# Whole rows and TensorE transposes for the first pair's q and k, forget gates on 96 partitions

## The chip, the cores and the metric

The kernel runs on one core of a Trainium2 chip. The metric is the device time of one execution in microseconds (us); the times before are the median of 3 runs.

## The reference

Three layers follow each other in fp32. The change touches the start of the first.

```python
# attention with forget gates: B, H, S, D = 4, 8, 576, 64
scores = (q @ k.transpose(0, 1, 3, 2)) / np.sqrt(D)
cum = np.cumsum(np.log(np.clip(f, 1e-4, 1.0)), axis=-1)
scores = np.where(causal, -1e9, scores + cum[:, :, :, None] - cum[:, :, None, :])
attn = softmax(scores)                       # causal masks the future
x = (attn @ v).transpose(0, 2, 1, 3).reshape(B * S, H * D)   # 2304 x 512

# a feed-forward layer, 512 -> 2048 -> 512, with a quadratic activation g
x = g(x @ w_in) @ w_out

# a top-1 mixture of 8 experts, 512 -> 1024 -> 512
out[n] = gate[n] * (relu(x[n] @ w1[e[n]]) @ w2[e[n]])
```

## The kernel before

The kernel is written as processes (Python generators) that a planner, the class `Order`, runs against a clock of its own: each step names an engine, a cost, a function that issues its instructions, and a rank; the lowest rank that is ready on an engine goes first. The order in which the functions are called is the order of the program on each engine's queue, so the planner's costs and due times decide the order, while on the chip each instruction waits for its real inputs. What a planner's gap on TensorE leaves open, `keep_warm` (L746 and after) fills with matmuls on the identity; every second turn issues one, and the first turn comes when `setup` is over, which costs 3000 ns on the planner's clock.

Attention goes over 16 pairs of heads. A pair has five units (blocks of 128 queries, in the order 4, 3, 2, 1, 0; block 4 holds the last 64 queries of both heads, and `corner` on GpSimd lays its q out in `qz`). A `unit` takes one of two score banks in PSUM (`SR` and `SRx`, two slots each), TensorE writes the scores into it and, for the first four pairs, adds the decays to them by a second set of matmuls (`sums`): pair 0 takes them from `cum` itself, pairs 1 to 3 from `parts`, which `sum_parts` makes from `cum`, later pairs by adding rows that have gone through DRAM (`rows`). Then `head` reads the bank on VectorE (L606), takes the exponential on ScalarE (L611), scales on GpSimd (L623) and turns the probabilities on TensorE (L637). `weighted` multiplies them with v.

The decays come from `forget_rows`: the gates are loaded four times, into 4 x 32 partitions of `cum` (L366), clamped (L370), their logarithm is taken (L372), scaled by -8 (L374) and summed along the sequence by a scan (L378). Before the scan it waits for `first_kt`, that is, for k of pair 0 to be turned.

q and k of a pair come by `load` (L411), four DMAs each on SP's queue, in pieces of 32 elements, and `turned` turns them by one VectorE transpose each (L464). Pair 1's DMAs wait, on the planner's clock, for pair 0's k. All of `attention` waits for the event `sums_there` before its first unit.

Beside attention the planner runs the first half of the feed-forward layer as soon as blocks of x are there, and prepares its weights in 16 pieces (`float64_piece`: L846 the DMA, L855 to L872 the steps on ScalarE, VectorE and GpSimd), whose earliest times stand in `FIRST_WEIGHTS`. Then come the second half and the experts, which are matmuls in a steady order.

Of the kernel before, what the change touches and what calls it, by code (L numbers as in the profile page):

```python
# [18 lines left out]
P = 128  # L19
# [18 lines left out]
NQK = 3  # L38
NP_ = 8
NSUM = 4  # L40
FIRST_WEIGHTS = [6000.0 + 2700.0 * n for n in range(5)] + [20500.0 + 5200.0 * n for n in range(11)]
PACE = 8500.0
WARM_FROM, WARM = 1500.0, 0.6
# [148 lines left out]
def dve(n, fn, prio=5.0, fast=False):  # L192
    return Use("DVE", 144 + n * (0.6 if fast else 1.05), fn, prio)
# [31 lines left out]
def kernel(  # L225
# [71 lines left out]
    statt = ap.tile([P, 10, 10], F32, name="stat")  # L297
    stats = [statt[:, n] for n in range(10)]

    cum = ap.tile([P, S], F32, name="cum")  # L300
    parts = ap.tile([P, S], F32R, name="parts")
    pick = ap.tile([NH, P], F32, name="pick")
    picks = ap.tile([P, P * NSUM], F32R, name="picks")
    past = [ap.tile([P, n], F32, name=f"past{n}") for n in (512, S)]
# [4 lines left out]
    p_b, sr_b, t_b, x_b, pt_b, pt4_b, xt_b = (  # L309
        Buffers(NP_), Buffers(4), Buffers(2), Buffers(1), Buffers(4), Buffers(1), Buffers(2))  # L310
    rows_there = Event()
    clamped, scaled_ok, first_kt = Event(), Event(), Event()
    sums_there = Event()
    parts_there = Event()
    raw_ok = {(i, n): Event() for i in range(NP) for n in "qk"}
# [13 lines left out]
    for b in range(B):  # L329
        for n in range(b * S // TB, ((b + 1) * S - 1) // TB + 1):  # L330
            xs_ok[n].n += NPAIR
    raws, qkt, cms, vs, pt, pt4, xts = {}, {}, {}, {}, {}, {}, {}

    def setup():
        make_identity(nc, ident)
# [20 lines left out]
    def forget_rows():  # L356


        got = yield (p_b, 3)
        low, rest, mids = (ap.tile([P, S], F32, tag="P", name=n, bufs=NP_)  # L360
                           for n in ("low", "rest", "mids"))
        go(sum_parts(rest, mids, got))

        def loads():
            for p0 in range(0, P, NH):
                nc.scalar.dma_start(cum[p0:p0 + NH], f.rearrange("b h s -> (b h) s"))  # L366
        yield Use("DVE", 400, lambda: (nc.vector.memset(quarter, 0.25), nc.vector.memset(low, -8.0)), 0)
        go(ln_table())
        yield dma(4 * NH * S * 4, loads, 0, "ACT", k=4)
        yield dve(S, lambda: nc.vector.tensor_scalar(cum, cum, 1e-4, 1.0, ALU.max, ALU.min), 0, True)  # L370
        done(clamped)
        yield act(S, lambda: nc.scalar.activation(cum, cum, AF.Ln), 0)  # L372
        go(exp_table())
        yield dve(S, lambda: nc.vector.tensor_scalar(cum, cum, -8.0, None, ALU.mult), 0, True)  # L374
        done(scaled_ok)
        yield first_kt

        yield dve(S, lambda: nc.vector.tensor_tensor_scan(cum, low, cum, 0.0, ALU.max, ALU.add), 0)  # L378
        done(sums_there)
        yield dma(NH * S * 4, lambda: nc.sync.dma_start(rows, cum[:NH]), 2)  # L380
        done(rows_there)

    def sum_parts(rest, mids, got):
        mids = mids.bitcast(F32R)
        yield sums_there
        yield act(S, lambda: nc.scalar.copy(parts, cum), 0.9)
        yield dve(S, lambda: nc.vector.tensor_tensor(rest, cum, f32(parts), ALU.subtract), 0.9)
        yield act(S, lambda: nc.scalar.copy(mids, rest), 0.9)
        yield Use("ACT", 700, lambda: nc.scalar.copy(parts[NH:2 * NH], rest[NH:2 * NH]), 0.9)
        yield dve(S, lambda: nc.vector.tensor_tensor(rest, rest, f32(mids), ALU.subtract), 0.9)  # L390
        yield Use("ACT", 700, lambda: nc.scalar.copy(parts[2 * NH:3 * NH], rest[2 * NH:3 * NH]), 0.9)
        give(p_b, got)
        done(parts_there)

    def ln_table():
        yield 600.0
        yield Use("ACT", 1400, lambda: nc.scalar.activation(tiny, quarter, AF.Ln), 0)
# [4 lines left out]
    def load(i, n):  # L402
        b, hp = divmod(i, NPAIR)
        h0 = 2 * hp

        def put(src, n):
            t = ap.tile([P, S // 32, 32], F32, tag="raw" + n, name=f"raw{n}{i}", bufs=2)
            for j in range(2):
                for dh in range(2):
                    p0 = 64 * j + 32 * dh  # L410
                    nc.sync.dma_start(  # L411
                        t[p0:p0 + 32],
                        src[b, h0 + j, :, 32 * dh:32 * dh + 32].rearrange(
                            "(tb t) d -> t tb d", t=32))
            return t
        g = yield (raw_b[n], 1)
        if i == 1:
            yield raw_ok[0, "k"]
        elif i:
            yield sums_there  # L420
        t = yield dma(P * S * 6, lambda: put({"q": q, "k": k}[n], n),
                      4 if i > 1 else 0.5, k=4)
        raws[i, n] = (t, g)
        done(raw_ok[i, n])

    def loadv(i):
        b, hp = divmod(i, NPAIR)
# [14 lines left out]
    def prep():  # L442

        for i in range(NP):
            for n in "qk":
                go(load(i, n))
        for i in range(NP):
            g = yield (qk_b, 1)
            qkt[i] = ([ap.tile([P, S], F32, tag=f"{n}t{g[0]}", name=f"{n}t{i}") for n in "qk"],
                      qz[g[0]], g)  # L450
            go(turned(i, "q"))
            go(turned(i, "k"))

    def turned(i, n):

        pr = PREP if i else 0
        yield raw_ok[i, n]
        if i == 0:
            yield clamped if n == "q" else scaled_ok
        r, g = raws.pop((i, n))  # L460
        r = r.rearrange("p a b -> p (a b)")
        (qt, kt), z, _ = qkt[i]
        t = qt if n == "q" else kt
        yield dve(S, lambda: nc.vector.transpose(t, r), pr)  # L464
        give(raw_b[n], g)
        done(qk_ok[i])
        if i == 0 and n == "k":
            done(first_kt)
        if n == "q":
            def corner():  # L470
                for j in range(2):
                    p = slice(64 * j, 64 * j + 64)
                    nc.gpsimd.tensor_copy(z[p, p], qt[p, 512:S])
            yield Use("POOL", 500, corner, pr)
            done(qk_ok[i])
# [60 lines left out]

    def unit(i, c, started):

        yield qk_ok[i]
        heads = (None,) if c == 4 else (0, 1)  # L540
        gp_ = yield (p_b, len(heads))
        sl = yield (sr_b, ((0, 1), (2, 3)))
        bank = SR[sl[0] // 2]
        done(started)
        (qt, kt), z, _ = qkt[i]
        w = P * (c + 1) if c < 4 else S

        def scores():
            if c == 4:
                for n in range(2):  # L550
                    nc.tensor.matmul(bank[:, n, :S // 2], z, kt[:, S // 2 * n:S // 2 * (n + 1)],  # L551
                                     start=True, stop=i >= NSUM)
                return
            for j in range(2):
                p = slice(64 * j, 64 * j + 64)
                nc.tensor.matmul(bank[:, j, :w], qt[p, P * c:P * c + P], kt[p, :w],  # L556
                                 start=True, stop=i >= NSUM)

        def sums():
            n3 = 3 * NH  # L560
            if i == 0:
                for n in range(2):
                    if c == 4:
                        nc.tensor.matmul(bank[:, n, :S // 2], pick,
                                         cum[:NH, S // 2 * n:S // 2 * (n + 1)], start=False, stop=True)
                    else:
                        p = slice(64 * n, 64 * n + NH)
                        nc.tensor.matmul(bank[:, n, :w], ident[p, 65 * n:65 * n + 1].to_broadcast(
                            [NH, P]), cum[p, :w], start=False, stop=True)
                return  # L570
            if c == 4:
                for n in range(2):
                    nc.tensor.matmul(bank[:, n, :S // 2], picks[:n3, P * i:P * i + P],
                                     parts[:n3, S // 2 * n:S // 2 * (n + 1)], start=False, stop=True)
                return
            for j in range(2):
                h = 64 * (2 * i + j)
                nc.tensor.matmul(bank[:, j, :w], picks[:n3, h:h + 1].to_broadcast([n3, P]),
                                 parts[:n3, :w], start=False, stop=True)
        yield Use("PE", max(440, 1.72 * w), scores, 0.8, full=0.8)  # L580
        done(s_done[i])
        if i < NSUM:
            yield parts_there if i else sums_there
            yield Use("PE", mm(w if c < 4 else S // 2, 2) if i else 1.72 * w, sums, 0.8)
        yield cm_ok[i, c]
        st = stats[(5 * i + SEQ.index(c)) % len(stats)]
        summed, scaled = Event(len(heads)), Event()
        left = Event(len(heads))
        for n, j in enumerate(heads):
            p = ap.tile([P, S], F32, tag="P", name=f"P{i}_{j}{c}", bufs=NP_)  # L590
            go(head(i, j, c, p, [gp_[n]], bank, st, summed, scaled, left))
        yield left
        give(sr_b, sl)
# [1168 lines left out]
```

## Time and profile before

| | us |
|---|---|
| median of 3 runs | 851.88 |
| lowest and highest | 850.98, 852.60 |
| the profiled execution | 852.66 |
| its span, first to last instruction | 851.0 |
| TensorE busy | 833.0 |
| VectorE busy | 443.7 |
| ScalarE busy | 360.4 |
| GpSimd busy | 303.5 |

Busy times are of the profiled execution. PE is TensorE, PEld its loading of weights, DVE is VectorE, ACT ScalarE, POOL GpSimd, SP the engine whose queue issues most DMAs. Matmuls overlap, so a busy TensorE isn't one at its peak. An fp32 matmul stands in the trace as two instructions.

### The profile page before, as it was taken

How to read it: one execution, taken by the hardware profiler on the slowest of the kernel's cores; microseconds unless marked ns; L12 is line 12 of the kernel's file. 1: busy time of each engine (PE TensorE's matmuls, PEld its weight loads, DVE VectorE, ACT ScalarE, POOL GpSimd, SP SyncE). 2: the span in 40 equal slices, each digit the busy share in tenths (PEclk: the TensorE clock that was granted, in tenths of full speed). 3: DMA queues.
4: the chain of work that ended last, by engine and by line, in shares of the span. 5: the costliest groups of instructions: out<-in, count | busy, mean ns of one | idle time of the engine just before them, and what ended most of it. 6: DMA issues, size and time to landing. Idle time of an engine off the chain costs nothing.

```text
span 851.0 us, 14093 instructions
## 1 busy us (share of the span) xinstructions
PE 833.0 (98%) x4886; PEld 661.1 (78%) x4886; DVE 443.7 (52%) x1081; ACT 360.4 (42%) x845; POOL 303.5 (36%) x410
## 2 busy tenths in 40 slices
PE   8999999999999999999999999999999999999997
PEld 5656666877787798888788888888998888887685
DVE  6877886555645537665755345466544521212021
ACT  5677676556556635443543342423333211102110
POOL 3657886555445534444442122212210033000000
PEclk9999999999999999999999999999999999999999
DMA  9889786565324146234422135664432111631220
GB/s 165 167 158 217 173 192 130 138 121 121 112 73 130 43 161 104 74 111 137 146 76 76 62 111 161 195 197 125 145 120 75 49 50 50 248 124 50 99 75 26
DMA packets 152152, 101.89 MB, mean 120 GB/s; under 512 B 102883, under 2 KB 122083, under 8 KB 152081
## 3 DMA queue, kind: packets, MB, share of 16 engines
q1 hardware_dynamic: 148624, 95.30, 41.8%
q0 software_dynamic: 3120, 5.27, 2.1%
q8 instruction: 39, 0.64, 0.3%
q10 hardware_dynamic: 336, 0.43, 0.2%
q14 instruction: 33, 0.26, 0.1%
HBM read 76.86 MB, written 24.49 MB: 119 GB/s over the span
## 4 chain that ended last, share of the span: by engine, by line
PE 86%; DVE 4%; POOL 3%; DMA 3%; issue 2%; ACT 1%; SPq 0%; ACTq 0%; POOLq 0%; DVEq 0%
PE hm L917 12%; PE hr L917 12%; PE hp L917 10%; PE accp L1051 7%; PE accr L1051 6%; PE accBr L1051 6%; PE accm L1063 6%; PE accBm L1063 6%; PE SR L556 4%; PE T L637 3%; PE X L677 3%; PE accBp L1051 2%; PE gt L1267 1%; PE U L730 1%; PE SR L551 1%
## 5 line engine op out<-in xcount | busy, mean ns | idle before, releaser
L939 POOL TENSOR_TENSOR glr<-gr,ghr 128x512 fp32r<-128x512 f32 x36 | 48.2, 1338 | 148.8 <-PE accBr L1051 69.1
L917 PE MATMUL hr<-rx,wb 128*128 128x512 f32 (+1 forms) x384 | 89.6, 367 | 0.0
L623 POOL TENSOR_SCALAR P<-P,stat 128x512 f32<-128x512 f32 (+3 forms) x128 | 74.3, 594 | 40.1 <-DVE stat L619 20.8
L917 PE MATMUL hm<-mx,wm 128*128 128x512 f32 (+1 forms) x336 | 87.0, 379 | 0.0
L611 ACT ACTIVATE P<-P,stat 128x512 f32<-128x512 f32 (+3 forms) x128 | 71.3, 559 | 29.0 <-DVE stat L606 28.0
L948 DVE SCALAR_TENSOR_TENSOR glm<-hm,ghm 128x512 fp32r<-128x512 f32 x36 | 24.8, 689 | 103.5 <-PE accBm L1063 68.4
L947 ACT ACTIVATE ghm<-hm 128x512 fp32r<-128x512 f32 x36 | 21.6, 599 | 132.9 <-PE accBm L1063 120.7
L917 PEld LDWEIGHTS hr<-rx,wb 128*128 128x128 f32 x384 | 65.7, 188 | 13.1
L917 PEld LDWEIGHTS hm<-mx,wm 128*128 128x128 f32 x336 | 61.0, 188 | 14.9 <-issue 3.4
L939 POOL TENSOR_TENSOR glp<-gp,ghp 128x512 fp32r<-128x512 f32 x36 | 48.6, 1350 | 57.8 <-ACT ghp L938 31.9
L1051 PE MATMUL accp<-ghp,wa 128*128 128x256 f32 (+1 forms) x384 | 68.9, 307 | 0.0
L1051 PEld LDWEIGHTS accp<-ghp,wa 128*128 128x128 f32 x384 | 53.7, 190 | 6.0 <-issue 1.8
L637 PE MATMUL T<-ident,P 128*128 128x128 f32 x320 | 52.2, 279 | 3.3 <-POOL P L623 2.7
L606 DVE CUSTOM_DVE_ANT_0 P<-SR,cm 128x512 f32<-128x512 f32 (+3 forms) x92 | 43.2, 486 | 23.3 <-PE SR L556 18.3
L637 PEld LDWEIGHTS T<-ident,P 128*128 128x128 f32 x320 | 36.6, 140 | 17.9 <-POOL P L623 8.6
L933 DVE SCALAR_TENSOR_TENSOR gr<-tr 128x512 f32<-128x512 f32 x36 | 24.8, 689 | 47.1 <-POOL glr L939 27.1
L657 ACT COPY pt<-T 128x512 f32<-128x512 f32 (+2 forms) x96 | 35.2, 391 | 33.0 <-PE T L637 32.3
L1051 PE MATMUL accr<-ghr,wb 128*128 128x512 f32 (+1 forms) x160 | 47.0, 375 | 0.0
L929 ACT ACTIVATE tr<-hr,quarter 128x512 f32<-128x512 f32 x36 | 24.8, 688 | 51.9 <-PE hr L917 24.6
L1051 PE MATMUL accBr<-ghr,wb 128*128 128x512 f32 (+1 forms) x160 | 46.5, 372 | 0.0
L1063 PE MATMUL accm<-wm,ghm 128*128 128x512 f32 x144 | 46.3, 394 | 0.0
L1063 PE MATMUL accBm<-wm,ghm 128*128 128x512 f32 x144 | 45.8, 392 | 0.0
(348 smaller groups left out, 1842.7 us busy)
## 6 DMA issues: line engine op xcount, KB each, us to landing
cm<-rows SPq DMA_DIRECT2D x24, 256.0 KB, 4.7
rawq<-in_q_dram SPq DMA_DIRECT2D x64, 72.0 KB, 3.5
rawk<-in_k_dram SPq DMA_DIRECT2D x64, 72.0 KB, 3.3
xs<-xT SPq DMA_DIRECT2D x16, 288.0 KB, 2.2
x2n<-nat SPq DMA_DIRECT2D x18, 256.0 KB, 2.2
war<-in_moe_w_in_dram SPq DMA_DIRECT2D x8, 512.0 KB, 5.0
rawv<-in_v_dram SPq DMA_DIRECT2D x32, 128.0 KB, 3.1
war<-in_moe_w_out_dram SPq DMA_DIRECT2D x8, 512.0 KB, 4.2
```

The costliest lines, as they stand in the source:

```text
L556: nc.tensor.matmul(bank[:, j, :w], qt[p, P * c:P * c + P], kt[p, :w], start=True, stop=i >= NSUM)
L606: yield dve(w + 80, lambda: nc.vector.tensor_tensor_reduce(out=pv_, in0=so, in1=m, scale=-0.125, scalar=3e38, op0=ALU.add, op1=ALU.min, ac ...
L611: yield act(w, lambda: nc.scalar.activation(pw, pw, AF.Exp, bias=st[:, n:n + 1], scale=-1.0, accum_out=st[:, 2 + 2 * n:3 + 2 * n]), 1, 330)
L623: yield pool1(w, lambda: nc.gpsimd.tensor_scalar(pw, pw, st[:, 8 + n:9 + n], 1.0, ALU.mult, ALU.mult), 0)
L637: nc.tensor.transpose(T[:, P * n:P * n + P], p[:, P * kb:P * kb + P], ident)
L657: yield act(n, lambda: nc.scalar.copy(dh, src), 0)
L677: nc.tensor.matmul(X[D * j:D * j + D, P * kb:], vt[:, kb, j], pt[i, j][0][:, 512 * kb:512 * kb + 512 - P * kb], start=(kb == 0), stop=(kb ...
L917: nc.tensor.matmul(oo, a[:, c, cs], x[c], start=(ip == 0 and c == 0), stop=(ip == 2 and c == KC - 1))
L929: yield act(n, lambda: nc.scalar.activation(t, oo, AF.Relu, bias=quarter, scale=0.25), 2, 60)
L939: yield pool2(n, lambda: nc.gpsimd.tensor_tensor(gl, g, f32(gh), ALU.subtract), 1)
L1051: nc.tensor.matmul(acc[d][:, :w], b[:, fc, P * d:P * d + P], g, start=(fc == 0 and ip == 0 and (not narrow or d % 2 == 0)), stop=(fc == NF ...
L1063: nc.tensor.matmul(acc[a * (4 // na)], g[:, P * a:P * a + P], b[:, fc], start=(fc == 0 and ip == 0), stop=(fc == NF - 1 and ip == 2))
```

## The change

- **q and k of pair 0** are loaded by two DMAs each, one for each head, whole rows of 64 elements: 96 partitions of six rows. TensorE turns them, six transposes each, into the score banks `SR` (q) and `SRx` (k); VectorE copies q out, ScalarE k, both with the rows put back in order. The rows lie in a buffer of the turned probabilities (`pt`). The waits of pair 0's transposes for `clamped` and `scaled_ok` go.
- **The forget gates** are loaded three times instead of four: one DMA on SP's queue ahead of q and k, two on ScalarE's queue. Clamp, logarithm, scaling, scan and the casts run on 96 partitions.
- **The scan** no longer waits for `first_kt`.
- **Pair 0's units** start with the sums (`start=True`), as soon as `sums_there` is done and a bank is free, and add the scores to them; the rank of the scores is 0.7 instead of 0.8 there. The sums of pair 0 hand on at the time they are issued.
- **Pair 1's loads** of q and k wait for `sums_there` like those of later pairs.

The core of the diff:

```diff
+NBY = 1
...
     def forget_rows():
...
-        def loads():
-            for p0 in range(0, P, NH):
-                nc.scalar.dma_start(cum[p0:p0 + NH], f.rearrange("b h s -> (b h) s"))
+        def load(e, p0):
+            e.dma_start(cum0[p0:p0 + NH], f.rearrange("b h s -> (b h) s"))
+
+        def third():
+            yield dma(NH * S * 4, lambda: load(nc.sync, 2 * NH), 0)
+            done(there)
+
+        def two():
+            yield dma(2 * NH * S * 4, lambda: (load(nc.scalar, 0), load(nc.scalar, NH)), 0, "ACT", k=2)
+            done(there)
+        there = Event(2)
+        cum0, cum, low = cum_, cum_[:3 * NH], low[:3 * NH]
+        go(third())
         yield Use("DVE", 400, lambda: (nc.vector.memset(quarter, 0.25), nc.vector.memset(low, -8.0)), 0)
+        go(two())
         go(ln_table())
-        yield dma(4 * NH * S * 4, loads, 0, "ACT", k=4)
+        yield there
...
         done(scaled_ok)
-        yield first_kt
-
         yield dve(S, lambda: nc.vector.tensor_tensor_scan(cum, low, cum, 0.0, ALU.max, ALU.add), 0)
...
     def load(i, n):
...
-        if i == 1:
-            yield raw_ok[0, "k"]
-        elif i:
-            yield sums_there
+        yield sums_there
...
+    def load_rows(i):
+
+        b, hp = divmod(i, NPAIR)
+        g = yield (pt_b, 1)
+        t = ap.tile([P, 13 * P], F32, tag="pt", name=f"rows{i}", bufs=4)
+        left = rows_left[i] = Event(2 if i == 0 else 4)
+
+        def one(n, a):
+            r = t[:96, 768 * a:768 * a + 768].rearrange("p (m x) -> p m x", m=6)
+
+            def put():
+                for j in range(2):
+                    nc.sync.dma_start(r[:, :, D * j:D * j + D], (q, k)[a][b, 2 * hp + j].rearrange(
+                        "(p m) d -> p m d", m=6))
+            yield dma(P * S * 4, put, 0.5, k=2)
...
+    def turned_rows(i, n):
...
+        def turn(dst, a):
+            for m in range(3):
+                nc.tensor.transpose(dst[:, 96 * m:96 * m + 96],
+                                    r[:, 3 * a + m],
+                                    ident[:96, :96])
+        if i == 0:
+            sl = yield (sr_b, ((0, 1), (2, 3)))
+            bank = SR[sl[0] // 2]
+            yield Use("PE", mm(96, 6), lambda: (turn(bank[:, 0], 0), turn(bank[:, 1], 1)), pr)
+            done(rows_left[i])
+            src = bank[:, :, :288].rearrange("p a (m t) -> p a m t", t=96)
+            if n == "q":
+                yield dve(S, lambda: nc.vector.tensor_copy(t, src), pr)
+            else:
+                yield act(S, lambda: nc.scalar.copy(t, src), pr)
+            give(sr_b, sl)
+            return
...
     def unit(i, c, started):
 
-        yield qk_ok[i]
+        yield qk_ok[i] if i else sums_there
...
-                                 start=True, stop=i >= NSUM)
+                                 start=i > 0, stop=i == 0 or i >= NSUM)
...
-                            [NH, P]), cum[p, :w], start=False, stop=True)
+                            [NH, P]), cum[p, :w], start=True, stop=False)
...
-        yield Use("PE", max(440, 1.72 * w), scores, 0.8, full=0.8)
+        if i == 0:
+            yield Use("PE", 1.72 * w, sums, 0.8, after=lambda o: o.now)
+            yield qk_ok[i]
+        yield Use("PE", max(440, 1.72 * w), scores, 0.8 if i else 0.7, full=0.8)
         done(s_done[i])
-        if i < NSUM:
-            yield parts_there if i else sums_there
-            yield Use("PE", mm(w if c < 4 else S // 2, 2) if i else 1.72 * w, sums, 0.8)
+        if 0 < i < NSUM:
+            yield parts_there
+            yield Use("PE", mm(w if c < 4 else S // 2, 2), sums, 0.8)
```

## Rows read from the trace of the kernel before

**Rows 1.** Stretches: start:end and length, busy us (instructions) by engine, clock, DMA.
```profile
100.00:120.00 20.00, 18.16 (x144) 13.74 (x143) 18.35 (x47) 13.76 (x37) 17.18 (x22) 1.00 0.78 167
...
137.00:300.00 163.00, 162.05 (x1309) 128.53 (x1308) 92.31 (x313) 98.71 (x267) 85.11 (x153) 1.00 0.44 106
300.00:620.00 320.00, 318.67 (x1579) 265.22 (x1578) 181.04 (x312) 123.37 (x242) 101.43 (x85) 1.00 0.41 126
620.00:851.00 231.00, 224.62 (x1142) 181.52 (x1140) 61.88 (x144) 45.42 (x90) 25.55 (x26) 1.00 0.25 88
```

**Rows 2.** Chain of waits, 0 to 22 us: start us, us, what.
```profile
5.25 2.88 DMA rawk<-in_k_dram
...
9.18 1.21 PE SR L551 x4
10.39 1.06 PE SRx L556 x4
11.45 0.92 PE SR L564 x3
12.37 1.10 PE SRx L568 x4
...
14.10 0.85 PE SR L556 x4
14.94 0.63 PE warm L755 x2
15.57 0.84 PE SR L568 x4
...
19.37 0.59 PE T_None L637 x4
```

**Rows 3.** Order of time, 0 to 22 us, other engines: start us, us, engine, instruction.
```profile
6.16 0.46 DVE L370 TENSOR_SCALAR cum<-cum 128x576 f32<-128x576 f32 x1 [2.50 <-DMA cum<-in_f_dram]
...
7.37 0.46 DVE L374 TENSOR_SCALAR cum<-cum 128x576 f32<-128x576 f32 x1
7.37 0.83 POOL L473 COPY qz<-qt 64x64 f32<-64x64 f32 x2 [2.69 <-DVE qt L464]
...
8.96 1.32 DVE L378 TENSOR_TENSOR_SCAN cum<-low,cum 128x576 f32<-128x576 f32 x1
...
10.31 0.67 ACT L386 CAST parts<-cum 128x576 fp32r<-128x576 f32 x1 [1.45 <-DVE cum L378]
...
12.86 0.75 DVE L606 CUSTOM_DVE_ANT_0 P_None<-SR,past 128x576 f32<-128x576 f32 x1
...
16.46 0.56 DVE L606 CUSTOM_DVE_ANT_0 P<-SR,past 128x384 f32<-128x384 f32 x1 [0.81 <-PE SR L568]
...
21.01 0.52 POOL L473 COPY qz<-qt 64x64 f32<-64x64 f32 x2 [1.24 <-DVE stat L619]
```

**Rows 4.** Gate DMAs of ScalarE's queue, the second alone, the fourth alone.
```profile
L366 ACTq DMA_DIRECT2D cum<-in_f_dram x1: 493/493/493, 1.4 to 1.4; - x1
...
DMA to landing us min/median/max: 3.1/3.1/3.1
...
L366 ACTq DMA_DIRECT2D cum<-in_f_dram x1: 513/513/513, 2.4 to 2.4; - x1
...
DMA to landing us min/median/max: 3.6/3.6/3.6
```

**Rows 5.** SP's queue in order of time; landing of pair 0's v, issued 12.5 to 15.6.
```profile
0.91 2.03 SPq L411 DMA_DIRECT2D rawq<-in_q_dram  x4
3.33 2.39 SPq L411 DMA_DIRECT2D rawk<-in_k_dram  x4
...
DMA to landing us min/median/max: 2.5/2.7/2.9
```

**Rows 6.** Warm-up matmuls, 2 to 5.4 us and 5.95 to 7.8 us: ns min/median/max.
```profile
L755 PE MATMUL warm<-ident x9: 634/634/795, 1.5 to 5.1; 128*128 128x256 f32 x9
...
L755 PE MATMUL warm<-ident x10: 379/379/574, 5.5 to 7.7; 128*128 128x256 f32 x10
```

More of the change, by code (lines that the diff above doesn't have):

```diff
@@ L298 @@
     stats = [statt[:, n] for n in range(10)]
-    cum = ap.tile([P, S], F32, name="cum")
-    parts = ap.tile([P, S], F32R, name="parts")
+    cum_ = cum = ap.tile([P, S], F32, name="cum")
+    parts_ = parts = ap.tile([P, S], F32R, name="parts")
     pick = ap.tile([NH, P], F32, name="pick")
@@ L311 @@
     rows_there = Event()
-    clamped, scaled_ok, first_kt = Event(), Event(), Event()
+    clamped, scaled_ok = Event(), Event()
     sums_there = Event()
@@ L331 @@
             xs_ok[n].n += NPAIR
-    raws, qkt, cms, vs, pt, pt4, xts = {}, {}, {}, {}, {}, {}, {}
+    rows_left, raws, qkt, cms, vs, pt, pt4, xts = {}, {}, {}, {}, {}, {}, {}, {}
     def setup():
@@ L383, in sum_parts @@
     def sum_parts(rest, mids, got):
-        mids = mids.bitcast(F32R)
+        n3 = 3 * NH
+        cum, parts, rest, mids = cum_[:n3], parts_[:n3], rest[:n3], mids.bitcast(F32R)[:n3]
         yield sums_there
@@ L424, in load @@
         done(raw_ok[i, n])
+    def load_rows(i):
[10 more added lines that the diff above has]
+            yield dma(P * S * 4, put, 0.5, k=2)
+            raws[i, n] = r
+            done(raw_ok[i, n])
+        go(one("q", 0))
+        go(one("k", 1))
+        yield left
+        give(pt_b, g)
@@ new lines, in turned_rows, with half @@
+    def turned_rows(i, n):
+        pr = PREP if i else 0
+        yield raw_ok[i, n]
+        r = raws.pop((i, n))
+        (qt, kt), z, _ = qkt[i]
+        t = (qt if n == "q" else kt).rearrange("p (t a m) -> p a m t", a=2, m=3)
+        def turn(dst, a):
[15 more added lines that the diff above has]
+            return
+        both = Event(2)
+        def half(a):
+            gt = yield (t_b, 1)
+            T = psa.tile([P, 512], F32, tag=f"T{gt[0]}", name=f"T{n}{i}{a}", bufs=1)
+            yield Use("PE", mm(96, 3), lambda: turn(T, a), pr)
+            done(rows_left[i])
+            src = T[:, :288].rearrange("p (m t) -> p m t", t=96)
+            if a:
+                yield act(288, lambda: nc.scalar.copy(t[:, 1], src), pr)
+            else:
+                yield dve(288, lambda: nc.vector.tensor_copy(t[:, 0], src), pr)
+            give(t_b, gt)
+            done(both)
+        go(half(0))
+        go(half(1))
+        yield both
@@ L444, in prep @@
         for i in range(NP):
+            if i < NBY:
+                go(load_rows(i))
+                continue
             for n in "qk":
@@ L456, in turned @@
         pr = PREP if i else 0
[L457 to L461, printed above, removed]
-        (qt, kt), z, _ = qkt[i]
-        t = qt if n == "q" else kt
-        yield dve(S, lambda: nc.vector.transpose(t, r), pr)
-        give(raw_b[n], g)
+        (qt, kt), z, _ = qkt[i]
+        if i < NBY:
+            yield from turned_rows(i, n)
+        else:
+            yield raw_ok[i, n]
+            r, g = raws.pop((i, n))
+            r = r.rearrange("p a b -> p (a b)")
+            t = qt if n == "q" else kt
+            yield dve(S, lambda: nc.vector.transpose(t, r), pr)
+            give(raw_b[n], g)
         done(qk_ok[i])
-        if i == 0 and n == "k":
-            done(first_kt)
         if n == "q":
@@ L556, in scores @@
                 nc.tensor.matmul(bank[:, j, :w], qt[p, P * c:P * c + P], kt[p, :w],
-                                 start=True, stop=i >= NSUM)
+                                 start=i > 0, stop=i == 0 or i >= NSUM)
         def sums():
@@ L564, in sums @@
                         nc.tensor.matmul(bank[:, n, :S // 2], pick,
-                                         cum[:NH, S // 2 * n:S // 2 * (n + 1)], start=False, stop=True)
+                                         cum[:NH, S // 2 * n:S // 2 * (n + 1)], start=True, stop=False)
                     else:
```

## The prediction

> **What bounds the kernel now.** I read the stretches first, then the chain of waits of the first 22 us, then the engines and the DMAs in that stretch. The stretches [rows 1] say where a gain can live. From 137 us to the end TensorE has work for 162.05 of 163, 318.67 of 320 and 224.62 of 231 us: what is gained there must be work taken from TensorE, and the change takes none. Before that it is otherwise: in 100 to 120 us VectorE is busy 18.35 of 20 us, GpSimd 17.18 and TensorE 18.16, so several engines share the bound. The change touches the start only, and what it gains must be handed on through that shared stretch as work already done.
>
> At the start the chain [rows 2] shows one thing ending last: k of pair 0, whose DMAs land at 5.25 + 2.88 = 8.13 us, is turned on VectorE, and the first score matmul starts at 9.18. From there the chain stays on TensorE: scores of block 4 (1.21), scores of block 3 (1.06), sums of block 4 (0.92), sums of block 3 (1.10). The decays wait longer than they must: the scan starts at 8.96 [rows 3], though its input was scaled by 7.37 + 0.46 = 7.83, because the order puts it behind k's transpose. Block 4's first read of the bank is at 12.86, block 2's at 16.46. Between the scores and the sums of block 2 (14.10 and 15.57) stands a warm-up matmul of 0.63 us: an order written with a gap between the two parts fills it.
>
> **The change part by part.** The profiled execution took 852.66 us, of which 851.0 are span and 1.66 lie around it; it is 0.78 us above the median of 851.88. I work out a lead on the span and take it from the median, which is the same as 852.66 less the lead less 0.78.
>
> *Forget gates.* Before, four DMAs of 72 KB stand on ScalarE's queue; the fourth is issued at 2.4 us and lands 3.6 us later [rows 4], at 6.0, and the clamp follows at 6.16 [rows 3]. After, two stand there and the third is the first on SP's queue. The second on ScalarE's queue goes out at 1.4 and landed after 3.1 us [rows 4], at 4.5; the one on SP takes the place of the first q DMA, issued at 0.91 [rows 5], and by the same times lands before that. Clamp at 4.6, so 1.55 us earlier. Bounds: 1.1 earlier if the second one takes the 3.6 us of the fourth, and 2.2 if lighter traffic takes 0.7 us from its 3.1. The third DMA costs SP one issue in front of q, about 0.5 us [rows 5].
>
> A rule of the Trainium skill speaks against this part: the page "DMA: Bandwidth & Descriptors", section "Issuing engines are not separate DMA queues", says that issuing from several engines saves only the time of issuing. By that rule the second queue gains one issue, some 0.5 us, and the rest of the 1.55 must come from the quarter that is no longer loaded; the trace before has each tensor on one queue and does not show it.
>
> *Scan.* From the clamp's start to the end of the scaling is 7.83 - 6.16 = 1.67 us, the scan takes 1.32 [rows 3]; 96 instead of 128 partitions change neither. It no longer waits for k. So the sums are there at 4.6 + 1.67 + 0.05 + 1.32 = 7.6 instead of 10.28, a lead of 2.6.
>
> *q and k in rows.* SP issues five DMAs instead of eight, at about 0.5 us each [rows 5], so q's last leaves at 2.4 and k's last at 3.4; before, k's last was out at 3.33 + 2.39 = 5.7. No trace row has these DMAs of 144 KB in pieces of 256 B; the nearest are v's, whose pieces are of 256 B too and which land 2.5 to 2.9 us after the issue [rows 5], and at the other end the 3.6 us of a gate DMA under the traffic of the start [rows 4]. q is there at 4.4 to 5.5, taken 5.0; k at 5.4 to 6.9, taken 6.4, instead of 8.13. Each is turned by six transposes; four of the 128-wide kind take 0.59 us on the chain [rows 2], so 0.9 for six, 1.8 if TensorE has its lower clock. Done by 6.8 and 8.2 at the latest, they lie before the sums or beside the scan.
> Two copies out of the banks come in and two transposes on VectorE go. q's copy is on VectorE, 576 wide from a bank as the first read at 12.86, so 0.75 us; by the planner's costs its turn is behind the scan (the scan is ready at 5.6 on its clock, the copy at 6.4). It runs 7.6 to 8.35. k's copy is on ScalarE behind the cast of the sums, 0.67 us each [rows 3]: 7.6 to 8.95. GpSimd's corner copy follows q's and takes 0.52 or, as at the start before, 0.83 us [rows 3]: done by 8.9 to 9.2. If q's copy came ahead of the scan instead, the sums would be 0.75 us later, and its bank free that much earlier.
>
> *Decays first.* The sums of block 4 need the bank that q was turned in, so they start at 8.4 and take 0.92, to 9.3. Then the scores of block 4, which also wait for the corner and for k's copy (9.2 at the latest): 9.3 to 10.5. Block 4 is read at 10.6 instead of 12.86. Then sums and scores of block 3, 1.10 + 1.06: done at 12.7; before, 12.37 + 1.10 = 13.47. Block 2's bank is free at about 11.4, its 0.84 + 0.85 follow at 12.7 without a warm-up matmul between: read at 14.5 instead of 16.46. So at full clock the lead at block 2 is 2.0 us (0.8 at block 3, 2.3 at block 4).
>
> *TensorE's clock.* This takes something back. The warm-up matmuls take 634 ns each before 5.5 us and 379 from then on [rows 6]: the engine stood at the lower level (1.2 GHz; the profile's clock row, which has no record so early, reads full) and rose to the full one at about 5.9, after 4.4 us of unbroken work since 1.5. The planner counts the transposes as TensorE's work and puts only what fits before q's data in front of them: by its order two warm-up matmuls instead of ten. On the chip these end at about 3.2, and TensorE stands idle till q lands. It may still be at the lower level at 8.4. Bounds: nothing, if the transposes and the few warm-up matmuls let it rise by then; 2.2 us, if it rises again only 4.4 us after the sums began, at 12.8, half of 4.4 being lost. I take 0.6: TensorE has work for well over half of 1.5 to 8.4, which is nearer to the unbroken row than to none. The lead is 2.0 - 0.6 = 1.4.
>
> *The rest.* Pair 1's q and k, pair 0's v and the sums' trip to DRAM move on SP's queue with the event that they follow; pair 1's DMAs can now run right behind pair 0's and be in k's way for part of a us, which the 6.9 above holds. ScalarE's two missing issues, VectorE's saved 0.8 us, the buffer that the rows borrow and the shorter casts cost nothing: they stand beside the DMAs of the first 8 us, or the buffer is back before the first probabilities are turned (19.37 on the chain [rows 2]).
>
> From pair 0 on I carry the 1.4 us to the end: TensorE's order is full, and in the shared stretch the weight pieces take what attention leaves on VectorE and GpSimd, so an earlier start is work done. The whole order after pair 0 is laid out anew, which can give or take about a us: the first 20 us alone hold stretches of filler of that size. 851.88 - 1.4 = 850.5.
>
> **The rivals.**
> *The clock comes late, slower.* If the clock stays low past 12.8, the loss passes the lead of 2.0 plus what the filler gives. The mechanism: each us of matmuls in the units of pair 0 at 1.2 GHz costs half a us. Rising only at 17 it costs (17 - 8.4) / 2 = 4.3 and leaves 2.3 lost: 854.2. It decides from a rise at about 12.5 on. For it: TensorE's gap from 3.2 to 5.0, and transposes in place of warm-up matmuls. Against it: once the sums start TensorE hardly waits, and 4.4 us of such work were enough before. The Trainium skill, "TensorE: Matmul & The Clock Gate", part 4 on PE-mode transposes, says that transposes do not bring the full clock as matmuls do; no row before has transposes at the lower level. Chance 0.15.
> *The lead is swallowed.* VectorE and GpSimd in 60 to 137 us, or a DMA that is queued as before, set when the weights of the first layer are ready, and the 1.4 us become a wait there. For it: 18.35 of 20 us on VectorE [rows 1]. Against it: the pieces follow free buffers, and attention's work is gone all the same. 851.6. Chance 0.19.
> *More is gained.* The clock is up in time (nothing lost of 2.0) and two gaps like the 0.63 at 14.94 go, so up to 3: 849.0. Chance 0.22.
> *It does not do what it says.* The rows, or the gates behind them, land no earlier than now, since TensorE's and ScalarE's new steps stand where VectorE's stood: 851.9. Chance 0.04.
>
> **How the numbers follow.** The forecast of 850.5 has 0.40, with 849.5 to 851.5 as its own range. A measurement of this kernel can tell about 0.2%, or 1.7 us, from no change, so the line is at 850.2 (and at 853.6 above). Of the forecast's 0.40 some 0.19 lie beyond it; with the 0.22 that is 0.41 for faster. The late clock at 854.2 reaches back over 853.6 in about a tenth of its cases, so slower is 0.14. The rest is 0.45. For 8 in 10 I reach down to 848.0, past which a quarter of the case of more lies (0.05), and up to 853.3, past which the late clock lies (0.14).
>
> **What would show it.** Right: the clamp near 4.6, the scan's end near 7.6, the sums of block 4 ahead of their scores, the first read of the bank near 10.6 and of block 2 near 14.5 us. The clock is read from the matmuls' own durations, as in rows 6: a first sum at about twice its time before means the lower level. The carry is read where TensorE becomes full at 137: if the same matmuls of the first layer stand there about 1.4 us earlier, it held. Wrong would be a scan that still ends after 9, matmuls at the lower level past 12.8, or a lead at 20 us that is gone at 137.

## The result, and the profile after

The changed kernel takes 858.69 us (median of 5 runs, 856.18 to 861.77), the kernel before 851.88 (5 runs, 850.98 to 852.6). The ratio is 1.0082, with a 95% interval of 1.0069 to 1.0096: slower, and outside the forecast's 848.0 to 853.3. The profiled execution took 861.77 us, its span 860.1. Executions of one kernel can differ by some us here, so where a profiled execution is far from its median, its own time is given.

TensorE's groups at the start, in order of time: start, duration, line, tiles, form, count, and the idle time before them.

```profile
1.52 2.07 PE L833 MATMUL warm<-ident 128*128 128x256 f32 x4 [1.52 <-POOL ident masks.py:199]
5.54 1.19 PE L466 MATMUL SR<-ident,rows 96*128 96x96 f32 x6 [1.94 <-DMA rows<-in_q_dram]
7.35 1.20 PE L466 MATMUL SRx<-ident,rows 96*128 96x96 f32 x6 [0.62 <-DMA rows<-in_k_dram]
8.34 1.11 PE L833 MATMUL warm<-ident 128*128 128x256 f32 x2
9.39 2.28 PE L639 MATMUL SR<-cum,pick 32*128 32x288 f32 x4
11.60 2.29 PE L626 MATMUL SR<-kt,qz 128*128 128x288 f32 x4
13.82 2.08 PE L643 MATMUL SRx<-cum,ident 32*128 32x512 f32 x4
15.83 2.08 PE L631 MATMUL SRx<-kt,qt 64*128 64x512 f32 x4
17.84 1.22 PE L833 MATMUL warm<-ident 128*128 128x256 f32 x2
```

Two warm-up matmuls (four instructions), then 1.94 us idle until q lands, and from there everything takes twice its time: the scores of block 4 take 2.29 us where [rows 2] have 1.21, those of block 3 2.08 for 1.06. That is TensorE at 1.2 instead of 2.4 GHz. How long it lasts is read from the warm-up matmuls, as in [rows 6]: two views of them, from 5.5 to 29.9 us and from 30.2 to 60 us (ns min/median/max).

```profile
L833 PE MATMUL warm<-ident x14: 634/634/794, 8.3 to 29.6; 128*128 128x256 f32 x14
...
L833 PE MATMUL warm<-ident x19: 377/379/634, 29.6 to 55.5; 128*128 128x256 f32 x19
```

Up to 29.6 us none is under 634 ns; behind that the median is 379. The stretches (columns as in [rows 1]) show the same as counts:

```profile
10.00:30.00 20.00, 20.00 (x48) 9.47 (x47) 7.49 (x24) 7.13 (x18) 3.56 (x5) 1.00 0.56 102
31.00:60.00 29.00, 29.00 (x208) 18.82 (x206) 23.63 (x80) 20.50 (x60) 17.16 (x30) 1.00 0.73 150
129.30:132.50 3.20, 3.16 (x15) 3.16 (x16) 3.09 (x10) 1.77 (x6) 3.20 (x5) 0.50 0.50 153
```

TensorE is never idle from 10 to 30 us, and yet only 48 of its instructions begin there. The clock column reads 1.00 in that stretch; it has no record before the rise and can't be believed there. At 129.3 it has one, a short second stretch at half the clock.

The other engines do their part of the change early, in order of time:

```profile
4.06 0.46 DVE L382 TENSOR_SCALAR cum<-cum 96x576 f32<-96x576 f32 x1 [0.41 <-DMA cum<-in_f_dram]
...
5.75 1.35 DVE L388 TENSOR_TENSOR_SCAN cum<-low,cum 96x576 f32<-96x576 f32 x1
7.03 1.19 DVE L476 COPY qt<-SR 128x576 f32<-128x576 f32 x1
...
8.59 1.18 ACT L478 COPY kt<-SRx 128x576 f32<-128x576 f32 x1 [0.77 <-PE SRx L466]
...
14.05 0.76 DVE L684 CUSTOM_DVE_ANT_0 P_None<-SR,past 128x576 f32<-128x576 f32 x1 [2.32 <-PE SR L626]
...
22.27 0.56 DVE L684 CUSTOM_DVE_ANT_0 P<-SR,past 128x384 f32<-128x384 f32 x1 [2.94 <-PE SR L631]
```

The clamp is at 4.06 and the scan done at 7.1, against 6.16 and 10.28 in [rows 3]. But block 4 is first read at 14.05 instead of 12.86, and block 2 at 22.27 instead of 16.46. What was won before 8 us is lost several times over on TensorE.

### The profile page after: what moved, and what is told of

The parts are those of the page before. It is cut to its first block, busy times and chain, and to the rows that moved or that the text cites. A ratio compares the mean times of both kernels' runs of the same rounds, so it can differ in the third digit from the quotient of the medians.

```text
span 860.1 us, 14075 instructions
## 1 busy us (share of the span) xinstructions
PE 839.8 (98%) x4880; PEld 664.4 (77%) x4880; DVE 443.1 (52%) x1080; ACT 360.7 (42%) x846; POOL 306.8 (36%) x410
## 4 chain that ended last, share of the span: by engine, by line
PE 95%; DVE 1%; issue 1%; DMA 1%; POOL 1%; ACT 1%; SPq 1%; DVEq 0%; POOLq 0%; ACTq 0%
PE hp L995 12%; PE hm L995 12%; PE hr L995 12%; PE accp L1129 9%; PE accr L1129 6%; PE accBr L1129 6%; PE accm L1141 6%; PE accBm L1141 6%; PE SR L631 4%; PE T L715 4%; PE X L755 4%; PE accBp L1129 3%; PE U L808 2%; PE SR L626 2%; PE gt L1345 1%; PE warm L833 1%
## 5 line engine op out<-in xcount | busy, mean ns | idle before, releaser
L701 POOL TENSOR_SCALAR P<-P,stat 128x512 f32<-128x512 f32 (+3 forms) x128 | 79.9, 637 | 36.1 <-DVE stat L697 19.9
L1011 DVE SCALAR_TENSOR_TENSOR gp<-tp 128x512 f32<-128x512 f32 x36 | 32.0, 888 | 35.8 <-POOL glp L1017 34.4
L631 PE MATMUL SR<-kt,qt 64*128 64x128 f32 (+3 forms) x224 | 45.7, 485 | 1.8 <-DVE stat L684 1.8
```

The lines of the kernel that those rows point to most:

```text
L701: yield pool1(w, lambda: nc.gpsimd.tensor_scalar(pw, pw, st[:, 8 + n:9 + n], 1.0, ALU.mult, ALU.mult), 0)
L1011: yield dve(n, lambda: nc.vector.scalar_tensor_tensor(g, t, 0.5, t, ALU.min, ALU.mult), 2)
```

## The experiments

### More warm-up matmuls in the changed kernel

The theory: TensorE's level alone costs the time. The edit puts five more warm-up matmuls in front of q's transposes, seven instead of two, and moves nothing else.

```diff
-        odd = [False]
+        odd, more = [False], [6]
...
-                nc.tensor.matmul(X[:, :2 * P], ident, two, start=True, stop=True)
+                for _ in range(more.pop() if more else 1):
+                    nc.tensor.matmul(X[:, :2 * P], ident, two, start=True, stop=True)
```

> The changed kernel with five more warm-up matmuls in the first turn, so seven stand before q's transposes instead of two; nothing else in any queue moves. Theory A (the clock): TensorE rises to the full clock near 5.9 us as before, pair 0's matmuls take half of what they take in the changed kernel, the first read of block 4 is near 11.5 instead of 14.05 us, block 2's near 15 instead of 22.3, and the time falls by 7 to 9 us, to 849 to 852. Theory B (the new order after pair 0 costs the time, the clock little): the first reads move as in A, but the time stays above 856. Theory C (warm-up matmuls don't lift the clock here, since transposes follow them): matmuls of pair 0 stay at 0.79 us a piece and the time stays at 858.

Measured: 850.78 us (849.86 to 851.8), ratio to the kernel before 0.9974 [0.9947, 1.0002]. One of the 25 executions of the kernel before beside it took 862.79 us, at a mean granted clock of 0.984, and widens that interval; the others lie between 850.83 and 853.46, with a median of 852.32 over all. TensorE in order of time:

```profile
1.52 5.83 PE L834 MATMUL warm<-ident 128*128 128x256 f32 x14 [1.52 <-POOL ident masks.py:199]
7.20 0.66 PE L466 MATMUL SR<-ident,rows 96*128 96x96 f32 x6
...
9.13 1.23 PE L639 MATMUL SR<-cum,pick 32*128 32x288 f32 x4 [0.32 <-DVE qt L476]
10.29 1.24 PE L626 MATMUL SR<-kt,qz 128*128 128x288 f32 x4
...
12.52 1.13 PE L631 MATMUL SRx<-kt,qt 64*128 64x512 f32 x4
```

The same matmuls take half the time, though q's transposes start 1.7 us later. Five matmuls that compute nothing are worth 7.9 us of median. The two orders are the same, so the loss can be followed to the end by the matmuls with v (first and last start; the changed kernel first, then this one):

```profile
L755 PE MATMUL X<-pt,rawv x256: 272/432/644, 41.3 to 310.0; 128*64 128x384 f32 x33, 128*64 128x512 f32 x32, 128*64 128x128 f32 x32, 128*64 128x256 f32 x31
```

```profile
L755 PE MATMUL X<-pt,rawv x256: 272/432/644, 31.3 to 299.3; 128*64 128x384 f32 x33, 128*64 128x512 f32 x32, 128*64 128x128 f32 x32, 128*64 128x256 f32 x31
```

10.0 us apart at the first, 10.7 at the last, 10.7 between the spans (860.1 and 849.4). From 8.34 to about 30.2 us TensorE worked 21.9 us at half the clock; half of that is 10.9. So 10.0 of the 10.7 us arise there, and they are carried to the end.

### Fewer warm-up matmuls in the kernel before

The counter-test, without any part of the change: two warm-up matmuls ahead instead of ten.

```diff
-        odd = [False]
+        odd, turn = [False], [0]
...
-                nc.tensor.matmul(X[:, :2 * P], ident, two, start=True, stop=True)
+                turn[0] += 1
+                if not 2 < turn[0] <= 10:
+                    nc.tensor.matmul(X[:, :2 * P], ident, two, start=True, stop=True)
```

> The kernel before, with two instead of ten warm-up matmuls ahead of its first scores; no order but that changes. Theory A: the clock stays at the lower level through pair 0, as in the changed kernel, so the old kernel loses what the changed one lost: block 2's first read near 23 instead of 16.5 us, time 858 to 862. Theory B: a loss of at most 2 us (853 to 854), since the clock rises again 4.4 us after the first scores.

Measured: 859.34 us (855.64 to 864.88), ratio 1.008 [1.0044, 1.0115]: by the medians as much as the change loses, without the change. The profiled execution, one of the shortest, took 856.39:

```profile
1.52 2.08 PE L757 MATMUL warm<-ident 128*128 128x256 f32 x4 [1.52 <-POOL ident masks.py:199]
9.31 2.26 PE L551 MATMUL SR<-kt,qz 128*128 128x288 f32 x4 [5.71 <-DVE kt L464]
11.50 1.72 PE L556 MATMUL SRx<-kt,qt 64*128 64x512 f32 x4
```

Here the level rises at about 12.7 us, in the middle of the second group. How much of it reaches the end is read from the last matmuls of the program (first and last start; the kernel before first, then this one):

```profile
L1063 PE MATMUL accBm<-wm,glm x72: 388/389/393, 646.1 to 844.2; 128*128 128x512 f32 x72
```

```profile
L1065 PE MATMUL accBm<-wm,glm x72: 388/390/394, 647.7 to 845.8; 128*128 128x512 f32 x72
```

They start 1.6 us later, about half of the 3.4 us that TensorE worked at the lower level; the other 2.1 of the 3.7 us between the spans (854.7 and 851.0) lie behind the last matmul. There is no transpose by TensorE ahead of these scores. So this execution shows that idling alone keeps the level low at the start, at a price of 1.6 us. The longer executions, up to 864.88, were not traced: that they lose the rest by the same level is likely, and not shown.

### The decays first, q and k as before

The gates, the scan and the sums-first order of the change stay; q and k of pair 0 come and are turned as before. The planner then puts six warm-up matmuls ahead.

```diff
-NBY = 1
+NBY = 0
...
-        yield sums_there
+        if i:
+            yield sums_there
```

> The changed kernel with pair 0's q and k loaded in pieces and turned by VectorE as before; gates on 96 partitions by two queues, the scan without its wait and the sums ahead of the scores stay. By its order six warm-up matmuls stand before the first sums. Theory A: if six keep the clock up to the rise (they fill TensorE till about 6.1 us) the gates and the decays alone show their worth: first read of block 4 near 11.5, time 850 to 851.5. If the clock is still at the lower level at the first sums, 857 to 860 as the changed kernel. Theory B (the new order of the rest costs): above 855 with the clock up.

Measured: 858.24 us (852.45 to 860.8), ratio 1.0062 [1.0028, 1.0096]. TensorE in order of time, in an execution of 856.03:

```profile
1.52 4.84 PE L834 MATMUL warm<-ident 128*128 128x256 f32 x12 [1.52 <-POOL ident masks.py:199]
8.08 1.43 PE L640 MATMUL SR<-cum,pick 32*128 32x288 f32 x4 [1.71 <-DVE cum L388]
9.44 2.29 PE L627 MATMUL SR<-kt,qz 128*128 128x288 f32 x4
```

Its stretch behind that, columns as in [rows 1]:

```profile
9.10:26.00 16.90, 16.90 (x42) 7.76 (x42) 7.48 (x24) 7.11 (x16) 2.54 (x3) 0.50 0.67 127
```

The level had risen, TensorE idled 1.71 us, and 1 us into the sums the level fell (1.43, then 2.29 us). The clock column has a record here, 0.50 up to 26 us. Nine of the ten executions have a mean granted clock of 0.986 to 0.990 and took 855.31 to 860.8 us; the tenth has 0.996 and took 852.45. So neither the rows nor TensorE's transposes are needed for the loss: with the old q and k, turned by VectorE, by these figures it came in nine of ten executions, and in the traced one behind idle time in front of the sums.

### The decays first, q and k as before, ten warm-up matmuls

The same kernel with four more of them ahead.

```diff
-        odd = [False]
+        odd, more = [False], [5]
...
+                for _ in range(more.pop() if more else 1):
```

> Gates on 96 partitions by two queues, scan and sums first, but pair 0's q and k in pieces and turned by VectorE as before; ten warm-up matmuls ahead of the first sums, so TensorE has no gap till then. Theory A: the clock is up from 5.9 us on and stays, where the same kernel with six fell back at 9.0; time 850 to 851. If the rows carry the gain of the changed kernel at full clock, 852 or more; if the gates and decays carry it, 850 to 851 as with rows.

Measured: 849.76 us (848.6 to 851.19), ratio 0.9973 [0.9962, 0.9984], the one version here whose interval lies wholly below 1. TensorE and VectorE in order of time:

```profile
1.53 6.93 PE L835 MATMUL warm<-ident 128*128 128x256 f32 x20 [1.53 <-POOL ident masks.py:199]
8.39 1.23 PE L640 MATMUL SR<-cum,pick 32*128 32x288 f32 x4
9.56 1.24 PE L627 MATMUL SR<-kt,qz 128*128 128x288 f32 x4
...
10.95 0.76 DVE L685 CUSTOM_DVE_ANT_0 P_None<-SR,past 128x576 f32<-128x576 f32 x1 [1.55 <-PE SR L627]
...
14.65 0.56 DVE L685 CUSTOM_DVE_ANT_0 P<-SR,past 128x384 f32<-128x384 f32 x1 [0.24 <-PE SR L632]
```

There is no gap; the sums start at 8.39, block 4 is first read at 10.95 and block 2 at 14.65. The gain of the change lies in the gates and the order of the decays. Six and ten warm-up matmuls are the only difference between this kernel and the one above, so the two also price the level without rows and without TensorE's transposes, by the matmuls with v (six first, then ten):

```profile
L756 PE MATMUL X<-pt,rawv x256: 272/432/644, 37.1 to 308.0; 128*64 128x256 f32 x33, 128*64 128x512 f32 x32, 128*64 128x384 f32 x32, 128*64 128x128 f32 x31
```

```profile
L756 PE MATMUL X<-pt,rawv x256: 272/432/644, 29.4 to 301.9; 128*64 128x256 f32 x33, 128*64 128x512 f32 x32, 128*64 128x384 f32 x32, 128*64 128x128 f32 x31
```

They are 7.7 us apart at the first, 6.1 at the last, and the spans 6.0 (854.4 and 848.4).

### Five warm-up matmuls instead of seven

In the first experiment's kernel seven warm-up matmuls hold up q's transposes: they start at 7.20, though q is there at about 5.5. Here `more = [False], [4]` leaves five.

> Edit: as the changed kernel with more warm-ups, but five instead of seven in front of q's transposes (the changed kernel has two). They end near 6.0 us, q is there at 5.5, so TensorE is busy from 1.5 to q's transposes without a gap but for the wait for k near 7.2. Theory of the clock (TensorE must not stand idle before the level has risen; seven ahead showed the rise at 6.7): the level rises near 6 us, the transposes take 0.66 us a six, q is copied about 1.0 us earlier than with seven (6.9 instead of 7.89), and the time is 850.0 to 850.8, the same as with seven or up to 0.8 better. Rival (the gap for k, or the narrow sums behind it, loses the level again as with the old q and k and six ahead, where it fell at 9.0 after a gap of 1.7 us): sums of block 4 at 2.2 us, low till 25 us or so, 856 to 859.

Measured: 850.9 us (849.79 to 858.29), ratio 0.9975 [0.9949, 1.0001]. By the median the theory held, and nothing more is won than with seven. Ten of the eleven executions took 849.79 to 852.86. The profiled one, though, took 858.29 and shows the rival, TensorE in order of time:

```profile
1.53 4.64 PE L834 MATMUL warm<-ident 128*128 128x256 f32 x10 [1.53 <-POOL ident masks.py:199]
5.95 0.89 PE L466 MATMUL SR<-ident,rows 96*128 96x96 f32 x6
7.74 0.69 PE L466 MATMUL SRx<-ident,rows 96*128 96x96 f32 x6 [0.90 <-DMA rows<-in_k_dram]
...
8.82 1.34 PE L639 MATMUL SR<-cum,pick 32*128 32x288 f32 x4
10.09 2.29 PE L626 MATMUL SR<-kt,qz 128*128 128x288 f32 x4
```

Its stretch behind that:

```profile
10.00:26.80 16.80, 16.80 (x39) 7.28 (x39) 7.00 (x23) 6.43 (x16) 2.54 (x3) 0.50 0.64 124
```

One program, and two courses of it: where the level is lost after the wait for k, the execution takes 7.4 us more than the median, a little under half of those 17 us. With five it can go either way; what tips it is open.

### The rows and TensorE's transposes alone

The kernel before with the rows, the transposes by TensorE and the two copies; gates, scan and order stay. Six warm-up matmuls stand ahead, so that the level is up at the start.

```diff
+NBY = 1
...
+            if i < NBY:
+                go(load_rows(i))
+                continue
...
+        if i < NBY:
+            yield from turned_rows(i, n)
```

> The kernel before with pair 0's q and k in whole rows, turned by TensorE and copied out; gates, the scan's wait and the scores ahead of the sums as before. Six warm-up matmuls ahead of q's transposes, one between, five behind, so TensorE has few gaps. If the rows carry the gain: below 851. If they give nothing, since the copies out of the banks take 1.19 us each where I reckoned 0.75 and the gates land later: 851.5 to 853. If the clock falls here: above 855.

Measured: 856.95 us (854.3 to 857.17), ratio 1.0044 [1.0028, 1.0059]: slower. The start, in order of time:

```profile
7.58 1.28 ACT L401 ACT_TABLE_LOAD   x1
8.99 1.17 ACT L471 COPY kt<-SRx 128x576 f32<-128x576 f32 x1
...
10.26 1.21 PE L621 MATMUL SR<-kt,qz 128*128 128x288 f32 x4
```

k is in its bank at about 8.0, but its copy stands behind the load of ScalarE's table and takes 1.17 us: scores at 10.26 instead of 9.18 [rows 2]. Block 2 is read at 18.84 instead of 16.46, so 2.4 of the 4.4 us between the spans (855.4 and 851.0) are there by then; from 86.6 to 93.2 us this execution shows half the clock, TensorE busy for 5.15 of it. The two executions with the highest granted clock (0.998 and 0.999) took 854.3 and 855.06, still 2.4 to 3.2 above the 851.87 of the kernel before beside them and above the 853 that was expected at most with the clock up: the slower start costs by itself. The copy's place holds for this edit alone; in the change the table is loaded earlier.

### The copies in reading order

The two copies write every sixth element, to put the rows back in order. In the first experiment's kernel they now write in the order in which they read.

```diff
-        t = (qt if n == "q" else kt).rearrange("p (t a m) -> p a m t", a=2, m=3)
+        t = (qt if n == "q" else kt).rearrange("p (a m t) -> p a m t", a=2, m=3)
```

> The changed kernel with seven warm-up matmuls in front; the two copies out of the banks write their 576 elements in the order in which they read them, so q and k stand in the wrong order and the scores are of other pairs of rows. It asks for the copies' own price. If the order of writing (every sixth element) makes them long, 0.70 to 0.75 us on VectorE and 0.65 to 0.70 on ScalarE; if it is the reading out of two banks, 1.19 us as now. The time: at most 0.5 us below the same kernel with the rows in order.

Measured: 851.33 us, one run. The copies in it:

```profile
7.67 0.76 DVE L476 COPY qt<-SR 128x576 f32<-128x576 f32 x1 [0.83 <-PE SR L466]
8.46 0.64 ACT L478 COPY kt<-SRx 128x576 f32<-128x576 f32 x1 [0.92 <-PE SRx L466]
```

0.76 and 0.64 us instead of 1.18 and 1.19: the reckoned prices were those of copies in order; the writing in steps of six costs 0.4 and 0.55 more. The first read moves from 11.77 to 11.37, and the end of that one run shows nothing of it.

### The gates on one queue

In the kernel with ten warm-up matmuls the third gate DMA goes on ScalarE's queue too.

```diff
-            yield dma(NH * S * 4, lambda: load(nc.sync, 2 * NH), 0)
+            yield dma(NH * S * 4, lambda: load(nc.scalar, 2 * NH), 0)
```

> Edit: on the kernel with the decays first, old q and k and ten warm-ups ahead (849.76 us, clamp of the gates at 4.30), the third gate DMA goes on ScalarE's queue like the other two; the planner's order is left as it is. Theory by the Trainium skill's rule on issuing (a second queue saves one issue, 0.45 us here): clamp at 4.75, the scan 0.45 later if it is not held by q's transpose; the time 0.0 to 0.5 us longer, 849.8 to 850.3, which three rounds can't tell from no change. Rival (a queue is served as a unit, as the fourth DMA of the kernel before, 3.6 us from issue to landing): clamp at 5.3 or later, one us, 850.7. Second rival: the gate DMAs are held by the common traffic, not by their queue, and with q's four DMAs issued 0.45 us earlier nothing is left of it: clamp within 0.2 of 4.30.

Measured: 851.92 us (850.82 to 858.17), ratio 1.0009 [0.9989, 1.0029]. The issues and the clamp:

```profile
0.90 1.50 ACTq L366 DMA_DIRECT2D cum<-in_f_dram  x3
...
5.08 0.46 DVE L382 TENSOR_SCALAR cum<-cum 96x576 f32<-96x576 f32 x1 [1.43 <-DMA cum<-in_f_dram]
```

The clamp goes from 4.30 to 5.08, between the two expectations: the last issue starts 0.5 us later (1.9 instead of 1.4), the rest is landing. The sums start 0.33 later (8.72), and TensorE's last matmuls 0.1 (841.7 and 841.6), so next to nothing of it reaches the end. The medians are 2.2 apart all the same: 0.5 of that lies between the two sets of runs (the kernel before took 852.36 beside this run and 851.87 beside the other), and two of the ten executions took 856.68 and 858.17 at a granted clock of 0.990 and 0.991, where the others have 0.997 or 0.998. The rest is open.

### Warm-up matmuls for longer

The first experiment's kernel has a short second stretch at half the clock, like the one at 129.3 above. Here the planner may fill gaps with warm-up matmuls until the next stage's first blocks are there.

```diff
-        go(keep_warm(xs_ok[0]))
+        go(keep_warm(half0.x_ok[1]))
```

> The changed kernel with seven warm-up matmuls in front, as before, and keep_warm running until block 1 of x is loaded (near 140 us) instead of block 0 (near 75). Theory A (the clock): the lower level that stood in 119 to 123 us of the profile with seven matmuls goes, and since TensorE then had work, half of its 3.4 us, 1 to 1.7 us, is gained: 849.0 to 849.8. Rival: the gap there is a wait for GpSimd and VectorE, the slow matmuls lie beside it, and nothing or up to 1 us is lost to warm-up matmuls in the way: 850.5 to 852.

Measured: 853.8 us (852.89 to 854.93), ratio 1.0023 [1.0012, 1.0034]. The two stretches, of the first experiment's kernel and then of this one:

```profile
100.00:120.00 20.00, 16.31 (x126) 12.16 (x125) 17.53 (x42) 12.16 (x30) 15.27 (x20) 0.98 0.77 191
120.00:122.00 2.00, 2.00 (x11) 2.00 (x11) 2.00 (x5) 1.77 (x6) 2.00 (x4) 0.50 0.49 174
```

```profile
120.00:140.00 20.00, 19.18 (x141) 14.14 (x140) 15.77 (x46) 14.23 (x40) 15.86 (x24) 1.00 0.56 141
```

The stretch at half the clock is gone and the kernel is slower, above both expectations. It has 72 warm-up instructions instead of 54 and another order. The last of the first layer's matmuls on `px0h` starts at 136.9 instead of 135.3, so 1.6 of the 2.7 us between the spans (852.1 and 849.4) are there by then. Whether the filler or the new order costs them is not shown.

## Why the prediction was wrong

- **TensorE's clock** is the step that failed. The mechanism stood there, with the two warm-up matmuls and the gap, and was priced at 0.6 us with 2.2 as the far end. It cost 7.9 us by the medians and 10.7 in the profiled execution. The far end rested on one row: that 4.4 us of work had brought the level before. The changed kernel worked from 9.39 to about 30 us without a gap and was at 1.2 GHz all that time. One rise, seen under one kind of work, was taken as a rule for another.
- **The rival "the clock comes late"** had the right cause and the right sign, with 0.15. Its price assumed a rise at 17 and gave 854.2. With the rise at 30.2 its own sum, (30.2 - 8.4) / 2 = 10.9, less the lead of 2.0 gives 860.8, against 861.77 for the profiled execution. The argument against it, that TensorE hardly waits once the sums start, was true and carried nothing. The transposes that the rival named in its favour are not needed: with the old q and k and six warm-up matmuls TensorE turns neither, and the level was low from 9.1 to 26 us all the same. The Trainium skill ("TensorE: Matmul & The Clock Gate", part 4 on PE-mode transposes) says that transposes do not bring the full clock as matmuls do. The after trace does not contradict it, since they took 1.19 us a six there and the level stayed low; but it was low before them, and with seven warm-up matmuls ahead the same six took 0.66.
- **Gates and scan**: right, a little too cautious. Clamp 4.06 for 4.6, scan done at 7.1 for 7.6, since the DMAs of ScalarE's queue landed 2.6 us after issue and not 3.1. The second queue is worth 0.78 us in the one-queue run (5.08 and 4.30), of which 0.5 is the issue. The other 1.08 are there with three DMAs on one queue (5.08 for the 6.16 of [rows 3]), so they go with the quarter that is no longer loaded. The Trainium skill ("DMA: Bandwidth & Descriptors", "Issuing engines are not separate DMA queues") says that issuing from several engines saves only the time of issuing; the run agrees for 0.5 of the 0.78.
- **q and k in rows**: q was there at 5.5, the end of its range, and k at about 7.2, past its 6.9: one issue of these DMAs took 0.61 to 0.73 us instead of 0.5. The bounds for the transposes' end, 6.8 and 8.2, were reckoned from the values taken and not from the ends of the ranges, which give 7.3 and 8.7; they ended at 6.73 and 8.55. The copies were mis-sized: 1.19 and 1.18 for 0.75 and 0.67. The row that was taken for q's copy reads a bank just as wide but writes in order.
- **Decays first**: right where the clock was held. With ten warm-up matmuls and the old q and k the sums start at 8.39 (reckoned 8.4), the first read is at 10.95 (10.6) and block 2's at 14.65 (14.5). With the rows and seven warm-up matmuls the first read is at 11.77, and block 2 is read at 16.01 for 14.5: the sums start 0.7 later behind the longer copy and the warm-ups, and one warm-up matmul of 0.63 still stands between blocks 3 and 2, which the sum had taken as gone.
- **The carry** held, for the loss: 10.0 us at the first matmul with v, 10.7 at the end. A gain was not simply carried: the kernel with ten warm-up matmuls leads by 1.8 us at block 2 and by 2.6 in the span (848.4), the one with rows and seven by 0.45 and by 1.6 (849.4), so about 1 us came behind block 2. Whether the new order gave it is not shown.
- **What the parts are worth.** At full clock the whole change has 0.9974 [0.9947, 1.0002], the decays alone 0.9973 [0.9962, 0.9984]; by the medians beside them that is 1.5 us (850.78 and 852.32) and 2.1 us (849.76 and 851.87). The rows add nothing that can be told, and alone they cost.

## What to carry to other kernels

A step that takes a wait off an engine's start also takes away the filler that was sized for that wait: look at what the planner counts as work, and price the idle time that appears. When the clock may be lost, bound the loss by half the time of the whole stretch of work at the start (here half of 21.9 us), and not by the one rise that a trace happens to show. An element count prices a copy only if the steps of both its sides are those of the row it is taken from.

## What was not expected of the hardware

- Unbroken work did not bring the full clock back for 20 us (9.4 to 29.6; the 14 warm-up instructions from 8.3 us on took 634 ns or more), while in the traced execution of the kernel before with two warm-up matmuls it rose at about 12.7, in the second group of its scores. The two starts differ in what the matmuls are, but that kernel's own times reach from 855.64 to 864.88, so its other executions have probably had other courses. What decides is open.
- A gap need not cost the level: the kernel before idles 0.92 us in front of its first scores and keeps it, the run with warm-up matmuls for longer idles 1.20 in front of k's transposes and keeps it, the run with five warm-up matmuls idles 0.90 in front of k's transposes and, in one course, loses it 2 us later. Both times the level was lost at the start (with the old q and k, and with five warm-ups), it came back at 26 to 27 us. In these two and in the changed kernel that was behind the sums and scores of the first four blocks, among the warm-up matmuls and the first transposes of probabilities that follow them; whether that is why is open.
- The kernel before is not safe from it either, it seems: one of 25 executions took 862.79 us at a mean granted clock of 0.984, and one of 19 took 861.62 at 0.987, where all others have 0.995 or more. Neither was traced.
- Copies out of PSUM with every sixth element written: 1.18 instead of 0.76 us on VectorE, 1.19 instead of 0.64 on ScalarE, for 128 x 576.
